# Where the first output tile's wo product is summed, when its head sums are read, and how the last output tile is cut

## The chip, the core and the metric

The kernel runs on one core of a Trainium2 chip. Five engines work side by side, each on its own instructions in its own order: TensorE (PE; its weight loads are listed as PEld), VectorE (DVE), ScalarE (ACT), GpSimd (POOL) and SyncE (SP), which here only issues transfers. They wait for one another through semaphores. The metric is device time in microseconds (us); lower is better. The kernel before takes 1537.7 us, the median of three runs from 1535.82 to 1538.98.

## What is computed

```python
mod = silu(c) @ w_mod                       # six rows of 640: sa, ca, ga, sb, cb, gb
h = layernorm(x) * (1 + ca) + sa            # x: 2048 x 640
q = h @ wq                                  # 32 heads of 128
p = softmax(q @ k_cache.T / sqrt(128))      # per head, 2048 keys
o = p @ v_cache
x = x + ga * (o @ wo)                       # o: 2048 x 4096, wo: 4096 x 640
h = layernorm(x) * (1 + cb) + sb
x1 = h + shift(gelu(layernorm(h) @ w1)) @ w2      # four groups of columns, shifted by 1, -1, 2, -2 tokens
h2 = gelu(layernorm(x1) @ w3) @ w4                # 640 -> 1728 -> 640
out = x + gb * (x1 + h2)
```

All inputs and the output are bf16; sums are in f32.

## The kernel before

The 2048 tokens are 16 tiles of 128. **Attention** runs over 512 steps `s`, head by head and in a head tile by tile (`h, j = divmod(s, 16)`). In a step PE multiplies the queries of tile `j` with all 2048 keys into the four banks of `Sps`, in two halves of 1024 columns (`qk`, L357 and L15). DVE copies each half to `negS`, negated and scaled, and keeps its minimum (L699). POOL takes the smaller of the two (L704), ACT the exponential of the row into a slot of `ring` (L707). The exponentials have to be transposed before they can be multiplied with the values: most of them by a DMA on SP for three steps at a time (a trio; `transpose`, L286), a few on PE (`t_piece`, L324, copied back by ACT, L331). Ten steps later (`PVD`) PE multiplies them with the values and a column of ones (`pv`, L371, 8 matmuls per half), and ACT copies the sums of two steps out of PSUM (L684). Four steps behind that POOL divides by the last column (L548, L555) and stores the result of four steps to `o_scratch` in DRAM (L562). So the loop has 526 rounds: steps 512 to 521 have no scores, only values.

`load_ot` (L604) reads `o_scratch` back for two tiles and a range of heads, transposed, into `OTj`, which lies in `hTx` for even pairs and in `negS` for odd ones. It is a DMA on SP's queue, so it takes its turn among the trios. Pair 0 (tiles 0 and 1) is read in three parts cut at `OTC = [0, 12, 31, 32]`: heads 0 to 11 in step 496, heads 12 to 30 in step 510 behind the last trio, head 31 in step 513. Each of the three lists the keys `HTK` (the old content of `hTx`) as written, so each waits for the landing of the part before. In step 513, SP also gets pair 1 in two halves of 16 heads, with the first four tiles of `x` (L612) between them; at step 522 the rest of `x`.

**The wo product** of tile 0 (`y0`, L643) is summed in the banks `Oaug` and `QPp`, that of tile 1 (`y1`, which calls `a_pe` on `Sps[:, 0:1024]`, L632) beside it; a head is one matmul of 512 and one of 128 columns. The table `TAIL` places pieces of them in the loop, behind the `pv` of a half step: in steps 506 to 511 (`Y0S = NG - 6`) one head of tile 0 per half step; in step 512 heads 0 to 7 of tile 1; in step 516 heads 8 to 11 of tile 1 and then heads 12 to 30 of tile 0. Behind the loop follow head 31 of tile 0, heads 12 to 31 of tile 1, and the other tiles by `a_pe` (tiles 2 to 5 in two halves of 16 heads, `a_two`). PE works strictly in this order: an instruction that waits holds up all that is listed behind it.

For each tile DVE then multiplies by `ga` (L757), adds `x` (L759), takes layernorm statistics (L749, L751; the root on POOL, L742, L744), modulates (L765, L768) and normalizes (L779); SP transposes the result (L785). The **MLP parts** follow with products L822 (w1), L885 (w2), L900 (w3) and L949 (w4), interleaved by a list.

The **last output tile** (tile 15, `e_last`) is worked in two halves of 320 columns: 14 matmuls each (L932) into two banks of the same `Sps` half, then on DVE a multiplication by `gb` (L915) and an addition (L918), then a store on SP (L921). `e_op` does the other tiles whole (L949; DVE L953, L955, L957; store L959). `ybank` hands out the two halves of `Sps` in turn.

`G.op` and `G.dma` record an operation with the keys that it reads (`r`) and writes (`w`); the waits are worked out from them, in the order of the program's text.

```python
Y0S = NG - 6
TAIL = {(s, z): [(y0, 2 * (s - Y0S) + z, 2 * (s - Y0S) + z + 1)] for s in range(Y0S, NG) for z in range(2)}
TAIL[(NG, 1)] = [(y1, 0, 8)]
TAIL[(NG + 4, 1)] = [(y1, 8, OTC[1]), (y0, OTC[1], OTC[2])]
```

Of the kernel before, what the change touches and what calls it, by code (L numbers as in the profile page):

```python
# [123 lines left out]
def bass_adaLN_cond__mha_block_cached__mixer_s_mlp__prompt_kernel(  # L124
# [21 lines left out]
    with ExitStack() as es:  # L146
# [9 lines left out]
        if True:  # L156
            with ExitStack() as es1:
# [445 lines left out]
                def load_ot(pr, h0=0, h1=H, part=0):  # L603
                    G.dma("sync", lambda e: e.dma_start_transpose(  # L604
                        OTj[pr % 2][:, 2 * h0:2 * h1, :], o_scr[pr, :, h0:h1].rearrange("q h z d -> q (h z d)")),
                          ("ot", pr % 2, part), r=[("osd", pr // 2, hh) for hh in range(h0, h1)],
                          w=[("OT", pr % 2, i) for i in ([part] if pr == 0 else (part, 2)[:part + 1] if h1 - h0 < H else range(3))]
                          + ([("OTa", 0)] if pr == 2 and part == 0 else [])
                          + (HTK if pr == 0 else NEG if pr == 1 and part == 0 else []))

                def load_xt(c0, c1):
                    G.dma("sync", lambda e: e.dma_start(  # L612
                        xt[:, 4 * c0:4 * c1], x2d[c0 * 512:c1 * 512, :].rearrange("(t p) d -> p t d", p=128)),
                        ("xt", c0), w=[("x1", t) for t in range(4 * c0, 4 * c1)] + ringk(XT0 + 4 * c0 * D, XT0 + 4 * c1 * D))

                OTC = [0, 12 * H // 32, H - 1, H]
                yn = [0]

                def ybank():
# [3 lines left out]
                def a_pe(j, b=None, parts=(0, 1, 2), hs=None):  # L623
                    if b is None:
                        b = ybank()
                    pr, z = divmod(j, 2)
                    h0, h1 = hs or (OTC[parts[0]], OTC[parts[-1] + 1])

                    def f(t):
                        for c0, cw in NC2:  # L630
                            for hh in range(h0, h1):
                                ins = t.matmul(YB[b][:, c0:c0 + cw], OTj[pr % 2][:, 2 * hh + z, :], wo[:, hh, c0:c0 + cw],  # L632
                                               start=(hh == 0), stop=(hh == H - 1))
                        return ins
                    G.op("tensor", f, r=[("OT", pr % 2, i) for i in parts] + [("OTa", pr % 2)] + ["wo", "woz", "wo4"],
                         w=[("S", b)] + ([("Sb", 2), ("Sb", 3)] if b == 1 else []))
                    return b

                def y0(h0, h1):
                    def f(t):  # L640
                        for jb, (c0, cw) in enumerate(NC2):
                            for hh in range(h0, h1):
                                ins = t.matmul(JB[jb][:, 0:cw], OTj[0][:, 2 * hh, :], wo[:, hh, c0:c0 + cw],  # L643
                                               start=(hh == 0), stop=(hh == H - 1))
                        return ins
                    G.op("tensor", f, r=[("OT", 0, i) for i in range(3) if OTC[i] < h1 and h0 < OTC[i + 1]] + [("OTa", 0), "wo", "woz", "wo4"],
                         w=[("J", 0), ("J", 1)])
# [7 lines left out]

                YB = [Sps[:, 0:1024], Sps[:, 1024:2048]]
                LAG = 4
                Y0S = NG - 6
                TAIL = {(s, z): [(y0, 2 * (s - Y0S) + z, 2 * (s - Y0S) + z + 1)] for s in range(Y0S, NG) for z in range(2)}
                TAIL[(NG, 1)] = [(y1, 0, 8)]  # L660
                TAIL[(NG + 4, 1)] = [(y1, 8, OTC[1]), (y0, OTC[1], OTC[2])]
                for s in range(NG + PVD + LAG):
                    h, j = divmod(s, NQT)
                    g_ = s - PVD
# [38 lines left out]
                    if s < NG:  # L703
                        G.op("gpsimd", lambda g, r8=r8: g.tensor_scalar(  # L704
                            out=nm[:, r8:r8 + 1], in0=nm0[:, r8:r8 + 1], scalar1=nm1[:, r8:r8 + 1], scalar2=None, op0=ALU.min),
                            r=[("nmh", 0, r8), ("nmh", 1, r8)], w=[("nm", r8)])
                        G.op("scalar", lambda a, s=s, r8=r8: a.activation(  # L707
                            ring[:, PSL[s], :], negS[:, s % 3, :], ACT.Exp, bias=nm[:, r8:r8 + 1], scale=-1.0),
                            r=[("negS", s % 3), ("nm", r8)], w=slot(PSL[s]))
                        for fn, *args in LATE.get(s, ()):  # L710
                            fn(*args)
                        if s in last_of:
                            transpose(last_of[s])
                        if j == 2 and h >= 1 and h + 1 < H:
                            load_k(h + 1)
                        if h + 1 == H and j in (0, NQT - 2):
                            i = int(j > 0)
                            load_ot(0, OTC[i], OTC[i + 1], i)
                        if j == (6 if h else 11) and h + 2 < H:
                            load_wq(h + 2)  # L720
                        if s == 9 and H > 1:
                            load_k(1)
                        if j == PVD + 1 and h + 1 < H:
                            load_v(h + 1)
# [117 lines left out]

                for i in range(NQT):
                    if i < NQT - 2:
                        b = (y0(OTC[2], H) or 0) if i == 0 else a_pe(1, 0, (1, 2)) if i == 1 else a_two(i) if i in (2, 3, 4, 5) else a_pe(i)
                    if i == NQT - 3:
                        for z in range(2):
                            G.op("gpsimd", lambda g, z=z: g.memset(us[:, :, z * SQ:z * SQ + 4], 0.0), w=[("usz", z)] + OT0K)  # L848
                    if i % 2 == 1 and (i + 3) // 2 < NQT // 2:
                        load_ot2((i + 3) // 2)  # L850
                    if i == 1:
                        G.dma("sync", lambda e: e.dma_start(w1, B_w1.rearrange("(k p) n -> p k n", p=128)), "w1", w=["w1"] + KVK)
                        G.dma("sync", lambda e: e.dma_start(w2, B_w2.rearrange("(k p) n -> p k n", p=128)), "w2", w=["w2"] + NEG)
                    if i < NQT - 2:
                        a_s1(i, b)
                    if 1 <= i:
                        a_s2(i - 1)
                    if 2 <= i:
                        nrm_of(1, i - 2)
                    if i == NQT - 2:  # L860
                        b = a_mixed(i, [[(b_op, 0, 0)], [(b_op, 0, 1)], [(b_op, 0, 2)], [(b_op, 0, 3)]])
                        a_s1(i, b)
                    if i == NQT - 1:
                        b = a_mixed(i, [[(b_op, 0, 4)], [(b_op, 1, 0)], [(b_op, 1, 1)], [(b_op, 1, 2)]])
                        nrm_of(1, i - 1)
                        a_s1(i, b)
                        a_s2(i)
                        nrm_of(1, i)
# [38 lines left out]
                def e_last(j):  # L907
                    b = ybank()
                    g = (j // 4) % 2
                    u = j % 2  # L910
                    q0 = (j % 4) * 128
                    for i in range(2):
                        c0 = i * HD
                        G.op("tensor", lambda t, i=i: e_half(t, b, g, q0, i), r=["w4", "w4b", "w4z", ("gT", g)], w=[("S", b, i)] + ([("S", b)] if i == 0 else []))
                        G.op("vector", lambda v, i=i, c0=c0: v.tensor_mul(  # L915
                            out=tmp[:, u, c0:c0 + HD], in0=YB[b][:, i * 512:i * 512 + HD], in1=mod_bc[:, 3 * D + c0:3 * D + c0 + HD]),
                            r=[("S", b, i), "mod"], w=[("tmp", u, i)] + ([("tmp", u)] if i == 0 else []))
                        G.op("vector", lambda v, c0=c0: v.tensor_add(  # L918
                            out=ob[:, u, c0:c0 + HD], in0=tmp[:, u, c0:c0 + HD], in1=xb[:, j, c0:c0 + HD]),
                            r=[("tmp", u, i), ("xb", j)], w=[("ob", u, i)] + ([("ob", u)] if i == 0 else []))  # L920
                        G.dma("sync", lambda e, c0=c0: e.dma_start(out2d[j * 128:(j + 1) * 128, c0:c0 + HD], ob[:, u, c0:c0 + HD]),  # L921
                              ("outl", i), r=[("ob", u, i)], w=[("ol", i)])

                def e_base(j):
# [2 lines left out]
                    G.op("vector", lambda v: v.tensor_add(out=xb[:, j], in0=xb[:, j], in1=xt[:, j]),  # L927
                         r=[("xb", j), ("x1", j)], w=[("xb", j)])

                def e_half(t, b, g, q0, i):  # L930
                    for f_ in range(NFT):
                        ins = t.matmul(YB[b][:, i * 512:i * 512 + HD], gT[g][:, f_, q0:q0 + 128],  # L932
                                       w4[:, f_, i * HD:(i + 1) * HD], start=(f_ == 0), stop=(f_ == NFT - 1))
                    return ins

                def e_op(j):
# [42 lines left out]
                    run_fill((2, 1, 1, 1, 2, 2, 1)[j] if j < 7 else 2)  # L979
                nrm_of(2, NQT - 1)  # L980
                run_fill(len(fill))
                G.flush("sync", [("ob", 0), ("ob", 1), ("ob", 1, 0), ("ob", 1, 1)])
                G.emit()


# [26 lines left out]
```

## Time and profile before

| | us |
|---|---|
| median of three runs | 1537.7 |
| the profiled execution | 1537.76 |
| its span, first to last instruction | 1536.0 |
| PE busy | 1473.2 (96%) |
| DVE busy | 1370.5 (89%) |
| ACT busy | 1257.6 (82%) |
| POOL busy | 625.8 (41%) |
| queue 1 (SP's transfers), share of 16 DMA engines | 100.7% |
| score steps end (last score matmuls) | 1210 |
| last `pv` matmuls end | 1239.6 |
| wo product of tile 15 ends | 1374.6 |
| last DVE operation ends | 1533.9 |

A busy share is a mean over stages that are limited by different things: in the score steps DVE works without a gap (its minimum of a half, 1222 ns, comes 1024 times), from 1240 us on PE does. The stretch of the edit lies between the two, from 1187 to 1263 us, where one stage runs out and the next has to be fed by transfers; the other edit touches the last 4 us. A matmul's listed length contains its way through the array, so the length of a stream of them is read from one start to another.

### The profile page before, as it was taken

How to read it: one execution, taken by the hardware profiler on the slowest of the kernel's cores; microseconds unless marked ns; L12 is line 12 of the kernel's file. 1: busy time of each engine (PE TensorE's matmuls, PEld its weight loads, DVE VectorE, ACT ScalarE, POOL GpSimd, SP SyncE). 2: the span in 40 equal slices, each digit the busy share in tenths (PEclk: the TensorE clock that was granted, in tenths of full speed). 3: DMA queues.
4: the chain of work that ended last, by engine and by line, in shares of the span. 5: the costliest groups of instructions: out<-in, count | busy, mean ns of one | idle time of the engine just before them, and what ended most of it. 6: DMA issues, size and time to landing. Idle time of an engine off the chain costs nothing.

```text
span 1536.0 us, 32447 instructions
## 1 busy us (share of the span) xinstructions
PE 1473.2 (96%) x13449; PEld 916.9 (60%) x12664; DVE 1370.5 (89%) x2424; ACT 1257.6 (82%) x1182; POOL 625.8 (41%) x1402
## 2 busy tenths in 40 slices
PE   6899999999999999999999999999999899999999
PEld 3466666666666666666666666666666565554545
DVE  8899999999999999999999999999999546668425
ACT  6999999999999999999999999999999600034230
POOL 1244444444444444444444444444444433333000
PEclk9999999999999999999999999999999999999999
DMA  9999999999999999999999999999999997624100
GB/s 331 244 231 252 231 250 235 236 234 248 243 247 242 239 241 237 246 234 249 231 251 235 244 232 250 232 239 235 246 233 243 231 242 165 142 74 116 35 22 35
DMA packets 1155088, 330.29 MB, mean 215 GB/s; under 512 B 1132986, under 2 KB 1149562, under 8 KB 1154938
## 3 DMA queue, kind: packets, MB, share of 16 engines
q1 hardware_dynamic: 1146448, 307.09, 100.7%
q0 software_dynamic: 6144, 16.79, 3.6%
q10 hardware_dynamic: 2346, 4.34, 0.8%
q8 instruction: 103, 1.69, 0.5%
q14 instruction: 47, 0.39, 0.1%
HBM read 43.48 MB, written 19.40 MB: 41 GB/s over the span
## 4 chain that ended last, share of the span: by engine, by line
ACT 62%; PE 19%; DVE 11%; DMA 4%; issue 3%; POOL 1%; SPq 0%; POOLq 0%; DVEq 0%
ACT ring L707 50%; DVE negS L699 10%; PE Sps L632 8%; ACT ring L331 4%; PE Sps L949 4%; ACT Of L684 3%; ACT kv L308 3%; DMA ring<-ring 2%; PE Oaug L900 2%; PE QPp L900 2%; PE Sps L885 1%; DMA ring<-in_A_x_dram 1%; PE PTp L371 1%; DMA kv<-Of 0%; DMA hTx<-o_scratch 0%
## 5 line engine op out<-in xcount | busy, mean ns | idle before, releaser
L699 DVE TENSOR_SCALAR_CACHE_REDUCE negS<-Sps 128x1024 f32<-128x1024 f32 x1024 | 1173.9, 1222 | 10.5 <-PE Sps L15 9.8
L707 ACT ACTIVATE ring<-negS,small 128x2048 bf16<-128x2048 f32 x512 | 1085.8, 2243 | 3.3 <-POOL small L704 3.2
L371 PEld LDWEIGHTS PTp<-kv,ring 128*128 128x128 bf16 x8192 | 557.4, 98 | 302.1 <-issue 75.7
L371 PE MATMUL PTp<-kv,ring 128*128 128x129 bf16 x8192 | 645.7, 221 | 11.4 <-DMA ring<-ring 10.4
L15 PE MATMUL Sps<-kv 128*128 128x512 bf16 x1007 | 383.0, 380 | 9.1 <-DVE negS L699 5.3
L704 POOL TENSOR_SCALAR small<-small 128x1 f32<-128x1 f32 x512 | 146.1, 285 | 598.1 <-DVE negS L699 598.0
L357 PE MATMUL Sps<-kv 128*128 128x512 bf16 x958 | 370.7, 387 | 14.5 <-DVE negS L699 2.4
L555 POOL TENSOR_SCALAR On<-Of,small 128x128 bf16<-128x128 f32 x512 | 190.1, 372 | 13.0
L357 PEld LDWEIGHTS Sps<-kv 128*128 128x128 bf16 x1024 | 98.3, 96 | 133.0 <-DVE negS L699 92.7
L684 ACT COPY Of<-PTp 128x259 f32<-128x259 f32 x256 | 153.3, 599 | 19.8 <-PE PTp L371 19.8
L548 POOL TENSOR_TENSOR small<-Of,small 128x4 f32<-128x4 f32 x128 | 133.1, 1040 | 18.4 <-ACT Of L684 18.3
L562 POOL DMA_DIRECT2D o_scratch<-On x128 | 103.8, 811 | 40.8 <-POOL On L555 37.2
L301 PE MATMUL Oaug<-hTx,kv 128*128 128x512 bf16 x254 | 96.3, 381 | 4.1 <-DMA kv<-in_A_wq_dram 2.4
L301 PE MATMUL QPp<-hTx,kv 128*128 128x512 bf16 x263 | 98.5, 382 | 1.1 <-ACT ring L331 0.8
L830 ACT ACT_TABLE_LOAD x1 | 1.3, 1283 | 109.9 <-POOL hTx L848 109.9
L699 DVE DVE_READ_ACCUMULATOR negS<-Sps 128x1 f32 x1024 | 87.2, 85 | 0.0
L742 POOL TENSOR_SCALAR negS<-negS 128x1 f32<-128x1 f32 x48 | 24.2, 504 | 121.8 <-DVE negS L751 121.8
L632 PE MATMUL Sps<-wo,negS 128*128 128x128 bf16 (+1 forms) x503 | 70.1, 298 | 0.5
L953 DVE TENSOR_TENSOR ring<-Sps,ring 128x640 f32<-128x640 f32 x15 | 12.4, 824 | 59.5 <-PE Sps L949 59.5
L331 ACT COPY ring<-QPp 128x512 f32<-128x512 f32 x78 | 63.8, 818 | 0.8 <-PE QPp L324 0.8
L331 ACT COPY ring<-Oaug 128x512 f32<-128x512 f32 x78 | 63.9, 819 | 0.0
L632 PE MATMUL Sps<-wo,hTx 128*128 128x512 bf16 (+1 forms) x441 | 60.8, 298 | 0.4
(108 smaller groups left out, 1053.1 us busy)
## 6 DMA issues: line engine op xcount, KB each, us to landing
kv<-in_A_v_cache_dram SPq DMA_DIRECT2D x32, 512.0 KB, 5.2
o_scratch<-On POOLq DMA_DIRECT2D x128, 128.0 KB, 5.6
kv<-in_A_wq_dram SPq DMA_DIRECT2D x32, 160.0 KB, 3.6
wo<-in_A_wo_dram SPq DMA_DIRECT2D x1, 5120.0 KB, 21.7
ring<-in_A_x_dram SPq DMA_DIRECT2D x5, 640.0 KB, 4.7
ring<-in_w_mod_dram SPq DMA_DIRECT2D x5, 640.0 KB, 8.6
out_dram<-wo SPq DMA_DIRECT2D x15, 160.0 KB, 1.8
ring<-ring SPq DMA_TRANSPOSE x144, 9.8
```

The source lines that it names most:

```text
L15: return t.add_instruction(mybir.InstMatmult(name=t.bass.get_next_instruction_name(), ins=[t.lower_ap(rhs), t.lower_ap(lhsT)], outs=[t.low ...
L301: G.op("tensor", lambda t: t.matmul(JB[jb], wq[:, hb, q, :], hT[:, q, cc * 512:(cc + 1) * 512], start=(q == 0), stop=(q == KT - 1)), r=[(" ...
L331: G.op("scalar", lambda a: a.copy(dst, src), r=keys[-1:], w=[("PT", TSL[g], r)])
L357: ins = (t.matmul if c2 == 0 else partial(same_weights, t))(Sps[:, col:col + 512], QT[:, hb, j * 128:(j + 1) * 128], KTs[:, hb, col:col + ...
L371: ins = t.matmul(ob[:, 0:129], pt, Vaug[:, hb, kt, 0:129], start=(kt == 0), stop=(kt == NKT - 1))
L548: G.op("gpsimd", lambda g: g.tensor_tensor(out=rl[:, 4 * b:4 * b + 4], in0=Of[:].rearrange("p a z d -> p (a z) d")[:, 4 * b:4 * b + 4, 128 ...
L555: G.op("gpsimd", lambda g: g.tensor_scalar(out=On[:, b, z, :], in0=Of[:, 2 * b + z // 2, z % 2, 0:128], scalar1=rl[:, 4 * b + z:4 * b + z ...
L632: ins = t.matmul(YB[b][:, c0:c0 + cw], OTj[pr % 2][:, 2 * hh + z, :], wo[:, hh, c0:c0 + cw], start=(hh == 0), stop=(hh == H - 1))
L684: G.op("scalar", lambda a, p=p: a.copy(Of[:, p % 4].rearrange("p z d -> p (z d)")[:, 0:259], PO[:, (p % 2) * 512:(p % 2) * 512 + 259]), r= ...
L699: G.op("vector", lambda v, half=half, dst=dst, src=src, r8=r8: v.tensor_scalar(out=dst, in0=src, scalar1=-SCALE, scalar2=None, op0=ALU.mul ...
L704: G.op("gpsimd", lambda g, r8=r8: g.tensor_scalar(out=nm[:, r8:r8 + 1], in0=nm0[:, r8:r8 + 1], scalar1=nm1[:, r8:r8 + 1], scalar2=None, op ...
L707: G.op("scalar", lambda a, s=s, r8=r8: a.activation(ring[:, PSL[s], :], negS[:, s % 3, :], ACT.Exp, bias=nm[:, r8:r8 + 1], scale=-1.0), r= ...
```

## The change

- `OTC` becomes `[0, 16, 31, 32]`: pair 0 is read as heads 0 to 15, 16 to 30, and 31.
- The second of these reads is issued in step 504 (`j == NQT - 8`) instead of 510: on SP's queue it stands behind the trio of steps 501 to 503 and ahead of those of 504 to 506 and 507 to 509.
- Only the first part writes the keys `HTK`; the other two no longer wait for the part before.
- `Y0S = NG - 8`: tile 0's heads 0 to 15 are summed in steps 504 to 511, one per half step.
- In step 513, behind its `pv` and `t_piece`, stand heads 16 to 30 of tile 0 and heads 0 to 30 of tile 1; the pieces of steps 512 and 516 are gone. Behind the loop only head 31 of both tiles is left.
- `e_last` takes three pieces of 320, 192 and 128 columns, the third in the other half of `Sps`; each has its 14 matmuls, two DVE operations and a store. `e_half` becomes `e_part`.

```diff
-                          + (HTK if pr == 0 else NEG if pr == 1 and part == 0 else []))
+                          + (HTK if pr == 0 and part == 0 else NEG if pr == 1 and part == 0 else []))
...
-                OTC = [0, 12 * H // 32, H - 1, H]
+                OTC = [0, H // 2, H - 1, H]
...
-                Y0S = NG - 6
+                Y0S = NG - 8
                 TAIL = {(s, z): [(y0, 2 * (s - Y0S) + z, 2 * (s - Y0S) + z + 1)] for s in range(Y0S, NG) for z in range(2)}
-                TAIL[(NG, 1)] = [(y1, 0, 8)]
-                TAIL[(NG + 4, 1)] = [(y1, 8, OTC[1]), (y0, OTC[1], OTC[2])]
+                TAIL[(NG + 1, 1)] = [(y0, OTC[1], OTC[2]), (y1, 0, OTC[2])]
...
-                        if h + 1 == H and j in (0, NQT - 2):
+                        if h + 1 == H and j in (0, NQT - 8):
                             i = int(j > 0)
                             load_ot(0, OTC[i], OTC[i + 1], i)
...
-                        b = (y0(OTC[2], H) or 0) if i == 0 else a_pe(1, 0, (1, 2)) if i == 1 else a_two(i) if i in (2, 3, 4, 5) else a_pe(i)
+                        b = (y0(OTC[2], H) or 0) if i == 0 else a_pe(1, 0, (2,)) if i == 1 else a_two(i) if i in (2, 3, 4, 5) else a_pe(i)
...
-                    for i in range(2):
-                        c0 = i * HD
-                        G.op("tensor", lambda t, i=i: e_half(t, b, g, q0, i), r=["w4", "w4b", "w4z", ("gT", g)], w=[("S", b, i)] + ([("S", b)] if i == 0 else []))
...
+                    b2 = ybank()
+                    for i, (c0, cw, dst, key) in enumerate([(0, 320, YB[b][:, 0:320], ("S", b)), (320, 192, YB[b][:, 512:704], ("S", b, 1)),
+                                                            (512, 128, YB[b2][:, 0:128], ("S", b2))]):
+                        G.op("tensor", lambda t, dst=dst, c0=c0, cw=cw: e_part(t, dst, g, q0, c0, cw), r=["w4", "w4b", "w4z", ("gT", g)], w=[key])
+                        G.op("vector", lambda v, c0=c0, cw=cw, dst=dst: v.tensor_mul(
+                            out=tmp[:, u, c0:c0 + cw], in0=dst, in1=mod_bc[:, 3 * D + c0:3 * D + c0 + cw]),
+                            r=[key, "mod"], w=[("tmp", u, i)] + ([("tmp", u)] if i == 0 else []))
+                        G.op("vector", lambda v, c0=c0, cw=cw: v.tensor_add(
+                            out=ob[:, u, c0:c0 + cw], in0=tmp[:, u, c0:c0 + cw], in1=xb[:, j, c0:c0 + cw]),
...
-                def e_half(t, b, g, q0, i):
+                def e_part(t, dst, g, q0, c0, cw):
                     for f_ in range(NFT):
-                        ins = t.matmul(YB[b][:, i * 512:i * 512 + HD], gT[g][:, f_, q0:q0 + 128],
-                                       w4[:, f_, i * HD:(i + 1) * HD], start=(f_ == 0), stop=(f_ == NFT - 1))
+                        ins = t.matmul(dst, gT[g][:, f_, q0:q0 + 128], w4[:, f_, c0:c0 + cw], start=(f_ == 0), stop=(f_ == NFT - 1))
```

## The prediction

> **What bounds the kernel now.** I read the shares and the chain of waits first, then the timelines of TensorE (PE) and of the DMA queue of SyncE (SP) where the edited lines run. Until 1206 us the chain is VectorE's (DVE) minimum over the scores; behind 1211 us it is almost only PE, with one long DMA in it:
>
> ```profile
> 1206.17 9.81 DMA ring<-ring
> ...
> 1220.37 7.22 DMA hTx<-o_scratch
> ...
> 1227.63 6.26 PE Oaug L643 x19
> 1233.89 1.06 PE QPp L643 x19
> ...
> 1262.78 8.64 PE Sps L632 x63
> ```
>
> Columns are start, length, what. L643 is `y0` (output tile 0 times wo, a 512- and a 128-column matmul per head), L632 is `a_pe` (the same for tile 1, here called `y1`, and later tiles); a whole tile of 32 heads takes 8.64 us, plus 0.05 of issue. The second read of head sums (L604, heads 12 to 30) is on the chain: PE waits for it. PE in order of time:
>
> ```profile
> 1192.84 0.63 PE L371 MATMUL PTp<-kv,ring 128*128 128x129 bf16 x8
> 1193.77 0.38 PE L15 MATMUL Sps<-kv 128*128 128x512 bf16 x1 [0.30 <-DVE negS L699]
> ...
> 1197.88 0.38 PE L643 MATMUL Oaug<-wo,hTx 128*128 128x512 bf16 x1
> ...
> 1210.08 0.38 PE L15 MATMUL Sps<-kv 128*128 128x512 bf16 x1
> ...
> 1211.04 1.10 PE L371 MATMUL PTp<-kv,ring 128*128 128x129 bf16 x16
> 1211.97 2.33 PE L632 MATMUL Sps<-wo,hTx 128*128 128x512 bf16 x16
> 1214.14 0.63 PE L371 MATMUL PTp<-kv,ring 128*128 128x129 bf16 x8
> ...
> 1216.02 0.64 PE L371 MATMUL PTp<-kv,ring 128*128 128x129 bf16 x8 [0.33 <-DMA ring<-ring]
> ...
> 1220.41 1.03 PE L632 MATMUL Sps<-wo,hTx 128*128 128x512 bf16 x7
> 1227.63 6.26 PE L643 MATMUL Oaug<-wo,hTx 128*128 128x512 bf16 x19 [6.19 <-DMA hTx<-o_scratch]
> ...
> 1234.79 4.85 PE L371 MATMUL PTp<-kv,ring 128*128 128x129 bf16 x80
> ...
> 1239.75 5.60 PE L632 MATMUL Sps<-wo,hTx 128*128 128x512 bf16 x40
> 1245.18 17.55 PE L632 MATMUL Sps<-wo,negS 128*128 128x512 bf16 x126
> ```
>
> Three things are to be seen: PE stands 6.19 us before 1227.63; the 40 matmuls of tile 1 (20 heads) come after that wait; and the first `y0` of the loop (step 506) runs at 1197.88 without waiting. The price of a head comes from the 40: 1245.18 - 1239.75 = 5.43 us for 20 heads, 0.2715 each. The 19 heads after the wait took 6.26 + 1.06 less an overlap, 1227.63 to 1234.79 = 7.16 us, where 19 x 0.2715 = 5.16: 2.0 us lost. The reason is the granted clock, here by windows (length, PE busy with its count, the other engines; then the clock; a view of PE alone has the clock third):
>
> ```profile
> 1221.50:1227.60 6.10, 0.00 (x0) 0.00 (x0) 0.00 (x0) 0.00 (x0) 0.00 (x0) 0.78 1.11 261
> ...
> 1532.07:1535.48 3.41, 0.73 (x6) 0.29 (x3) 1.63 (x4) 0.00 (x0) 0.00 (x0) 1.00 0.29 96
> 1535.48:1535.90 0.42, 0.00 (x0) 0.00 (x0) 0.00 (x0) 0.00 (x0) 0.00 (x0) 0.50 0.00 0
> ...
> 26.81:30.23 3.42, 1.90 (x14) 1.00 0.98 240
> ```
>
> It falls during the wait and is 0.50 again only at the very end of the program.
>
> SP works off its queue in order, nearly without a gap (start, length, queue; below it the wait list, and the time from issue to landing of the transposes that start at 1187.21, 1228.88 and 1235.13):
>
> ```profile
> 1187.21 5.03 SPq L604 DMA_TRANSPOSE hTx<-o_scratch  x1
> 1192.33 27.99 SPq L286 DMA_TRANSPOSE ring<-ring  x4
> 1220.37 8.46 SPq L604 DMA_TRANSPOSE hTx<-o_scratch  x2
> 1228.88 5.58 SPq L604 DMA_TRANSPOSE negS<-o_scratch  x1
> ...
> 1235.13 5.99 SPq L604 DMA_TRANSPOSE negS<-o_scratch  x1
> 1241.22 0.53 SPq L612 DMA_DIRECT2D ring<-in_A_x_dram  x1
> 1245.38 12.06 SPq L604 DMA_TRANSPOSE hTx<-o_scratch  x2
> ...
> SPq L109 <- DMA hTx<-o_scratch: 2.0, 1, 2.0
> ...
> hTx<-o_scratch SPq DMA_TRANSPOSE x1, 8.2
> ...
> negS<-o_scratch SPq DMA_TRANSPOSE x1, 7.6
> ...
> negS<-o_scratch SPq DMA_TRANSPOSE x1, 9.2
> ```
>
> The four trios cost 7.0 us of queue each, and the read of heads 12 to 30 stood behind all four.
>
> **Part by part. The wait at 1227.63 goes.** The read of heads 16 to 30 now stands ahead of the last two trios. SP: the first read (now 16 heads; 12 took 5.03, and 16 heads of another tile 5.58 to 5.99) ends near 1193.1, two trios 1207, the read is issued there. At 7.2 to 9.2 us it lands at 1214 to 1216. PE gets there (step 513, behind the values of steps 512 and 513, which take 0.93 + 1.40 us) not before 1213.4 + what the loop has lost; below that is 1216.7. So no wait, and the clock stays up: 6.19 + 2.0 us go. The 0.33 us ahead of 1216.02 goes as well: in its place stands the block of 15 heads of tile 0 and 31 of tile 1, 46 x 0.2715 = 12.5 us. Four heads of tile 0 (12 to 15) leave the stretch behind the loop for steps 504 to 507, 4 x 0.2715 = 1.09 us. The 19 heads of tile 1 that move from 1240 us into the block cost the same there. Removed: 6.19 + 2.0 + 0.33 + 1.09 = **9.6 us**.
>
> **What the moved reads delay.** The last two trios are issued near 1212 and 1219 in place of 1206.17 and 1213, and land (9.81 us in the chain) at 1222 and 1229. Behind the block PE wants them at 1229.2 and 1233.6. Hidden; without the block in front they would cost the 6 us. The wait of 2.0 us on SP goes, since the last read no longer waits for the landing of the one before it. So tile 2's two reads start at about 1227 and 1233.5 and land by 1235 and 1243.
>
> **A wait is added in step 504.** `y0` now starts two steps earlier, behind the eight matmuls of 1192.84, which leave PE at 1193.3 (8 at some 0.06 us). It needs the first read. That landed at 1187.21 + 8.2 = 1195.4 with 12 heads; with 16 I put it a third of its 5.03 us of queue at most, nothing at least, later (0 to 1.7), and take 1.0, the order of the difference to 5.99: 1196.4. PE so stands **3.1 us** (2.1 to 3.8). All behind it on PE wait: the second score half of step 504, hence DVE, ScalarE's exponentials and everything to the loop's end. It isn't made up: with `y0` in them the 14 halves between 1193.77 and 1210.08 took 16.31 us, 1.165 each, and those with `y0` are set by PE without a gap; the four halves of steps 504 and 505 join them for some 0.1 to 0.2 us. Added: **3.3 us**. SP is not held up: its trios are behind by then anyway.
>
> **Does this stall drop the clock?** In the rows a stretch of 3.41 us with 1.90 us of PE work kept it at 1.00 and one with 0.73 lost it. A stall of 3.1 us leaves between 0.3 and 1.9 us of work in the emptier of the two stretches that it touches, by where it falls. If it drops, some 3.4 us of loop run at half speed: 1.7 us more (the trace's own case: 2.0). I take no drop, for the stall that shows one is twice as long. The Trainium skill ("TensorE: Matmul & The Clock Gate", Part 1: The HAM clock gate) says that the clock falls after at least one whole idle window of about 3.4 us, the windows running freely; by that 3.1 us costs nothing and the sum stands. The row of 1532.07 speaks against the strict form of it, having 0.73 us of work in its window, which is why the drop is a rival below.
>
> **What comes after.** PE's way from 1211.04 to 1262.78 loses 9.6 and gains 3.3: tile 2 starts at 1238.9 instead of 1245.18, its second half at 1243.2, with its heads landed by 1243; tile 3 follows, tile 4 starts at 1256.5. Tile 4's two reads waited on SP until 1245.38 for tile 1's matmuls; now they go out near 1240.5, straight behind the transfer of the row of 1241.22, and their 12.06 us of queue end near 1252.5, where the two halves of tile 4 want them at 1256.5 and 1260.8. From there PE is the chain to the end, and the **6.3 us** stay.
>
> **Last tile in three pieces.** DVE:
>
> ```profile
> 1531.00 0.82 DVE L957 TENSOR_TENSOR wo<-ring 128x640 bf16<-128x640 f32 x1
> 1531.74 0.48 DVE L915 TENSOR_TENSOR ring<-Sps,mod_bc 128x320 f32<-128x320 f32 x1
> 1532.26 0.49 DVE L918 TENSOR_TENSOR wo<-ring 128x320 bf16<-128x320 f32 x1
> 1532.84 0.49 DVE L915 TENSOR_TENSOR ring<-Sps,mod_bc 128x320 f32<-128x320 f32 x1
> 1533.36 0.49 DVE L918 TENSOR_TENSOR wo<-ring 128x320 bf16<-128x320 f32 x1
> ...
> 1240.56 0.28 DVE L757 TENSOR_TENSOR ring<-QPp,mod_bc 128x128 f32<-128x128 f32 x1
> ```
>
> DVE, not PE, sets this end: it comes from the tile before without a gap, and waited only some 0.07 us for the second half. A start-to-start of 0.52 us for 320 columns and 0.31 for 128 gives 0.38 for 192. The first piece is over at 1532.78 as before; then 2 x 0.38 + 2 x 0.31 = 1.38 to 1534.16, where it was 1533.85: **0.3 us lost**. Bounds: 0.1 gained, if the third transfer, of 32 KB for 80, returns faster, to 0.5 lost.
>
> **Sum.** The profiled execution took 1537.76 us (its span 1536.0), the median of three is 1537.7. 1537.76 - 9.6 + 3.3 + 0.3 = **1531.8 us**, and as much against the median.
>
> **Rivals.** (1) The stall in step 504 drops the clock: 1.7 us more, 1533.5. For it, the row of 1532.07; against it, a stall shorter than the stretch of 3.41 us. (2) The stall is short or absent, the first read landing as early as before: PE gains up to 9.6, but then waits for the second half of tile 2's heads, which cannot land before 1244.3 less the 2.0 us of the SP wait; tile 4 starts at 1242.3 + 4.34 + 8.69 = 1255.3, 7.5 us earlier: 1530.6. For it only the small growth of the read. (3) The DMA engines and not SP's wait set tile 2's reads: they land at 1244.3 as before, and tile 4 starts at 1257.3: 1532.6. (4) Slower: the block of 92 matmuls stands in front of the values of the last eight steps, and all of them wait if the read of heads 16 to 30 is late. Behind its landing PE still has 12.5 + 4.4 + 4.9 + 0.6 = 22.4 us (block, values of steps 514 to 516, the 80 matmuls, the two last heads) up to tile 2, which began at 1245.18; so it decides from a landing at 1222.5 on, 15.5 us after its issue. A landing after 20 us would give 1227 + 22.4 + 2.0 of clock = 1251.4, 6.2 us late: 1544.3. Against it, all rows of L604 land within some 10 us. A landing a few us late only eats the gain: at 1221 the time is 1536.3.
>
> **How the numbers follow.** Forecast with (3), which differs by less than 1 us: 0.55; (1) 0.25; (2) 0.12; (4) 0.08, half of it past the point of no gain. The range goes from 1530.2, just below (2), to 1534.4, above (1) with the stall at its upper bound. What differs by less than 0.2% (3.1 us) can't be told from no change here; faster thus means under 1534.6, which the first three give but for the far end of (1): 0.9; the same 0.06; slower 0.04.
>
> **What would show it.** In the profile after: a PE wait of about 3 us for `hTx<-o_scratch` at 1193 us in the loop, at a clock of 1.00 behind it; no wait ahead of the block of 92 matmuls at about 1217; the last 80 values matmuls ending near 1238; tile 4 at 1256.5; the last DVE piece 1.38 us after the first. Wrong are my reasons if that first wait is missing, if the block stands waiting for its read, if the trios are waited for behind it, or if the gain of 6.3 us is gone by the MLP.

## The result, and the profile after

The changed kernel takes 1530.88 us, the median of six runs (1529.45 to 1532.75); the kernel before, beside it, 1537.5 (1534.63 to 1540.31). The ratio is 0.9959 with a 95% interval of 0.9945 to 0.9973, so 4.2 to 8.5 us of gain: faster, by more than the 0.2% named in the prediction, and 0.9 us under the forecast of 1531.8.

The profiled execution took 1530.71 us, its span 1528.9. Its span is 7.1 us shorter than that of before, but 1.6 us of this were there before the first edited instruction of PE: the first score matmul of step 504, just ahead of it, starts at 1190.81 us, before at 1192.39. A distance between two starts of one profile is free of that. From this matmul to the first one of tile 4 ("the stretch" from here on) before took 1262.78 - 1192.39 = 70.4 us, and the changed kernel 1255.41 - 1190.81 = **64.6 us**. The rest, to the end of the span, took 273.2 and 273.5.

The chain of waits of the changed kernel (start, length, what) through the edited part:

```profile
1185.66 8.63 DMA hTx<-o_scratch
1194.34 0.39 PE Oaug L643
...
1216.31 3.24 PE Oaug L643 x15
1219.55 0.84 PE QPp L643 x15
1220.39 8.42 PE Sps L632 x62
...
1232.96 4.68 PE PTp L371 x80
...
1237.91 32.21 PE Sps L632 x233
```

The DMA on the chain is now the first read, not the second. Behind it PE runs without a gap. The timeline of PE, same kernel:

```profile
1191.26 0.63 PE L371 MATMUL PTp<-kv,ring 128*128 128x129 bf16 x8
1194.34 0.39 PE L643 MATMUL Oaug<-wo,hTx 128*128 128x512 bf16 x1 [2.45 <-DMA hTx<-o_scratch]
...
1194.85 0.63 PE L15 MATMUL Sps<-kv 128*128 128x512 bf16 x1
...
1196.67 0.63 PE L357 MATMUL Sps<-kv 128*128 128x512 bf16 x1
...
1198.60 0.38 PE L357 MATMUL Sps<-kv 128*128 128x512 bf16 x1
...
1216.15 3.40 PE L643 MATMUL Oaug<-wo,hTx 128*128 128x512 bf16 x15
...
1228.64 0.63 PE L371 MATMUL PTp<-kv,ring 128*128 128x129 bf16 x8
...
1232.80 4.84 PE L371 MATMUL PTp<-kv,ring 128*128 128x129 bf16 x80
...
1238.02 17.55 PE L632 MATMUL Sps<-wo,negS 128*128 128x512 bf16 x128
1255.41 17.55 PE L632 MATMUL Sps<-wo,hTx 128*128 128x512 bf16 x128
```

Three things answer to the prediction. The wait of 6.19 us ahead of the 19 heads is gone, and the block starts at 1216.15 without one. A new wait of 2.45 us stands ahead of the first `y0` in step 504. And behind it score matmuls last 0.63 us instead of 0.38 until 1198.6. That is the clock, by two windows of 3.41 us (length, PE busy, the clock):

```profile
1191.49:1194.90 3.41, 0.96 (x11) 0.99 1.26 253
1194.90:1198.31 3.41, 3.41 (x22) 0.51 1.28 290
```

From one score half to the next it is 2.05 and 1.93 us in this time, where 1.17 is the rule: 1.64 us for the clock. The wait itself made the half of step 504 3.81 us long instead of 1.14 to 1.16: 2.65. (The wait is listed from the listed end of the matmuls before it, hence 2.45.) In all the loop from step 504 to its last score half takes 21.84 us (1190.81 to 1212.65) for 17.48 before (1192.39 to 1209.87), 4.4 lost; from there to tile 4 it takes 42.8 for 52.9, 10.1 won.

SP's queue in the same profile:

```profile
1185.66 5.50 SPq L604 DMA_TRANSPOSE hTx<-o_scratch  x1
1191.26 12.25 SPq L286 DMA_TRANSPOSE ring<-ring  x2
1203.55 5.41 SPq L604 DMA_TRANSPOSE hTx<-o_scratch  x1
1209.06 14.08 SPq L286 DMA_TRANSPOSE ring<-ring  x2
1223.29 1.17 SPq L604 DMA_TRANSPOSE hTx<-o_scratch  x1
1224.51 4.71 SPq L604 DMA_TRANSPOSE negS<-o_scratch  x1
...
1229.90 5.92 SPq L604 DMA_TRANSPOSE negS<-o_scratch  x1
```

The second read goes out at 1203.55 and is there (7.5 us) before PE asks; the last two trios, landing 9.8 and 10.4 us after their issue, are on time as well. The last tile on DVE:

```profile
1524.72 0.48 DVE L915 TENSOR_TENSOR ring<-Sps,mod_bc 128x320 f32<-128x320 f32 x1
1525.24 0.49 DVE L918 TENSOR_TENSOR wo<-ring 128x320 bf16<-128x320 f32 x1
1525.64 0.35 DVE L915 TENSOR_TENSOR ring<-Sps,mod_bc 128x192 f32<-128x192 f32 x1
1526.03 0.36 DVE L918 TENSOR_TENSOR wo<-ring 128x192 bf16<-128x192 f32 x1
1526.31 0.28 DVE L915 TENSOR_TENSOR ring<-Sps,mod_bc 128x128 f32<-128x128 f32 x1
1526.62 0.29 DVE L918 TENSOR_TENSOR wo<-ring 128x128 bf16<-128x128 f32 x1
```

2.19 us from the first of these to the end of the last (before 2.11), and 1.99 more to the end of the span (before 2.15): 4.18 for 4.26.

### The profile page after: what moved, and what is told of

Same layout as the page of the kernel before. It is cut to its first block, busy times and chain, and to the rows that moved or that the text cites. A ratio compares the mean times of both kernels' runs of the same rounds, so it can differ in the third digit from the quotient of the medians.

```text
span 1528.9 us, 32717 instructions
## 1 busy us (share of the span) xinstructions
PE 1489.2 (97%) x13702; PEld 918.8 (60%) x12678; DVE 1370.9 (90%) x2426; ACT 1258.5 (82%) x1182; POOL 627.0 (41%) x1402
## 4 chain that ended last, share of the span: by engine, by line
ACT 70%; PE 21%; DVE 4%; DMA 3%; issue 2%; SPq 1%; POOL 0%; DVEq 0%
ACT ring L706 57%; PE Sps L632 9%; ACT ring L331 4%; ACT Of L683 4%; ACT kv L308 4%; PE Sps L948 3%; DVE negS L698 3%; PE Oaug L899 2%; PE QPp L899 2%; PE PTp L371 1%; PE Sps L884 1%; DMA ring<-ring 1%; DMA kv<-in_A_wq_dram 1%; ACT hTx L473 1%; SPq L222 1%
## 5 line engine op out<-in xcount | busy, mean ns | idle before, releaser
L706 ACT ACTIVATE ring<-negS,small 128x2048 bf16<-128x2048 f32 x512 | 1112.7, 2355 | 5.3 <-POOL small L703 4.8
L357 PE MATMUL Sps<-kv 128*128 128x512 bf16 x1024 | 396.0, 387 | 8.1 <-DVE negS L698 3.6
L15 PE MATMUL Sps<-kv 128*128 128x512 bf16 x1024 | 389.2, 380 | 0.0
L683 ACT COPY Of<-PTp 128x259 f32<-128x259 f32 x256 | 181.6, 710 | 4.5 <-PE PTp L371 4.5
L301 PE MATMUL Oaug<-hTx,kv 128*128 128x512 bf16 x315 | 119.4, 381 | 4.8 <-DMA kv<-in_A_wq_dram 3.3
L301 PE MATMUL QPp<-hTx,kv 128*128 128x512 bf16 x325 | 121.3, 379 | 0.9 <-ACT ring L331 0.8
L331 ACT COPY ring<-QPp 128x512 f32<-128x512 f32 x78 | 73.1, 937 | 0.0
L331 ACT COPY ring<-Oaug 128x512 f32<-128x512 f32 x78 | 72.9, 935 | 0.0
```

The source lines that it names most:

```text
L15: return t.add_instruction(mybir.InstMatmult(name=t.bass.get_next_instruction_name(), ins=[t.lower_ap(rhs), t.lower_ap(lhsT)], outs=[t.low ...
L301: G.op("tensor", lambda t: t.matmul(JB[jb], wq[:, hb, q, :], hT[:, q, cc * 512:(cc + 1) * 512], start=(q == 0), stop=(q == KT - 1)), r=[(" ...
L331: G.op("scalar", lambda a: a.copy(dst, src), r=keys[-1:], w=[("PT", TSL[g], r)])
L357: ins = (t.matmul if c2 == 0 else partial(same_weights, t))(Sps[:, col:col + 512], QT[:, hb, j * 128:(j + 1) * 128], KTs[:, hb, col:col + ...
L683: G.op("scalar", lambda a, p=p: a.copy(Of[:, p % 4].rearrange("p z d -> p (z d)")[:, 0:259], PO[:, (p % 2) * 512:(p % 2) * 512 + 259]), r= ...
L706: G.op("scalar", lambda a, s=s, r8=r8: a.activation(ring[:, PSL[s], :], negS[:, s % 3, :], ACT.Exp, bias=nm[:, r8:r8 + 1], scale=-1.0), r= ...
```

## The experiments

All are edits of the changed kernel (the runs called again repeat a kernel). The theory: the order of the reads took away the wait and the cold clock behind it, and the price is the early `y0`, by its wait and by the clock. The stretch is read from each profile, and so is the distance from the same matmul to the end of the span, since what is won ahead of tile 4 can be lost behind it; times are medians, ratios are to the kernel before.

| run | stretch, us | to the end, us | time, us | ratio, 95% interval |
|---|---|---|---|---|
| before | 70.4 | 343.6 | 1537.5 | |
| changed | 64.6 | 338.1 | 1530.88 | 0.9959 (0.9945 to 0.9973) |
| changed, again | 64.8 | 338.2 | 1532.6 | 0.9962 (0.9947 to 0.9977) |
| e1: `y0` from step 506 | 62.7 | 336.9 | 1528.62 | 0.9949 (0.9937 to 0.9962) |
| e2: `y0` from step 505 | 62.0 | 336.7 | 1529.11 | 0.9952 (0.9940 to 0.9964) |
| e2 again (e11) | 63.0 | 338.2 | 1529.07 | 0.9942 (0.9927 to 0.9958) |
| e3: the wait filled | 63.3 | 337.0 | 1530.12 | 0.9962 (0.9946 to 0.9978) |
| e4: second read behind the trios | 75.7 | 349.2 | 1541.79 | 1.0035 (1.0021 to 1.0048) |
| e5: block in step 516 | 68.1 | 341.8 | 1534.3 (one run) | |
| e6: keys of the reads kept | 63.2 | 337.3 | 1530.01 (one run) | |
| e7: last tile in two halves | 61.6 | 335.5 | 1528.61 (one run) | |
| e8: e2, block begins with tile 1 | 62.3 | 335.6 | 1531.46 | 0.9964 (0.9952 to 0.9977) |
| e9: e1, first read of 12 heads | 65.3 | 338.8 | 1529.9 | 0.9960 (0.9948 to 0.9973) |

**The order of the reads (e4).**

```diff
-                        if h + 1 == H and j in (0, NQT - 8):
+                        if h + 1 == H and j in (0, NQT - 2):
```

> Edit: the changed kernel with the read of heads 16 to 30 back in step 510, behind the last two trios on SP. Theory (the order of the read is what pays): it is issued 14 us later and lands near 1225 on the scale of the changed kernel, PE waits 8.7 us ahead of the block and loses 2.0 to the clock: 75.3 us for the stretch, 10.7 us more time than the changed kernel and 4 to 5 more than before the change. Rival (what pays is the new place of tile 1's heads and the steps 504 and 505): 64.6, no loss.

PE's timeline in e4, the block's first matmuls:

```profile
1223.47 6.19 PE L643 MATMUL Oaug<-wo,hTx 128*128 128x512 bf16 x15 [10.22 <-DMA hTx<-o_scratch]
```

A wait of 10.22 us, and 15 heads at half clock. The stretch is 75.7 us where the theory had 75.3, and the kernel is slower than before the change. That the two numbers agree so well is luck: from the last score half to tile 4 it took 55.9 us for 42.8, 13.2 more where 10.7 was expected, and in the loop PE waited only 2.01 us and kept its clock, 2.1 less. With everything else of the change in place, the read's turn on SP decides between a gain and a loss.

**The wait and the clock in step 504 (e1, e2, e3).** e1 sets `Y0S = NG - 6` and begins the block with head 12 (`(y0, 12, OTC[2])`); e2 takes `NG - 7` and 14. e3 puts ten matmuls into the wait:

```diff
+                def busy(n):
+                    def f(t):
+                        for _ in range(n):
+                            ins = t.matmul(JB[0], wo[:, 0, 0:128], wo[:, 1, 0:512], start=True, stop=True)
+                        return ins
+                    G.op("tensor", f, r=["wo"], w=[("J", 0)])
+                TAIL[(Y0S, 0)] = [(busy, 10)] + TAIL[(Y0S, 0)]
```

> Edit: tile 0 is summed from step 506 on (heads 0 to 11, as before the change), heads 12 to 30 in the block of step 513; reads and the rest as in the changed kernel. Measured on PE from the first score matmul of step 504 to the first matmul of tile 4: before 70.4 us, changed 64.6. Theory (the wait in step 504, 2.6 us, and the clock drop behind it, about 1.65, are on the path): both go, four heads (1.1) come back into the block, so 61.4 us and 3.2 us less time than the changed kernel. Rival (the wait is absorbed, since the transfers set the end): 64.6 to 65.7, no gain.

> Edit: tile 0 is summed from step 505 on (heads 0 to 13), heads 14 to 30 in the block. Theory: the first read lands 3.5 us after the first score matmul of step 504, and the first y0 is now due 3.2 us after it: a wait of 0.3 us, no clock drop, two heads (0.5) back in the block: 61.2 us for the stretch that took 64.6. Rival (absorbed): 64.6 or more. A second rival (the wait is set by something other than the read's landing and moves along with y0): again a wait of 2.5 us and 64.6.

> Edit: the changed kernel with ten matmuls of 512 columns (2.15 us, their result is overwritten) ahead of the first y0 in step 504, where PE waits anyway. Theory (the clock drop is a cost of its own): the wait for the read shrinks to about 0.4 us, the end of the wait stays, the granted clock stays at 1.00, the stretch takes 62.9 us instead of 64.6. Rival (the drop costs nothing, since DVE or the transfers set the pace there): 64.6. Were the wait not for the read, it would be 2.15 us longer: 66.8.

The waits of PE, first e1, then e2, then e3:

```profile
1200.48 0.64 PE L371 MATMUL PTp<-kv,ring 128*128 128x129 bf16 x8 [0.73 <-DMA ring<-ring]
1212.20 4.28 PE L643 MATMUL Oaug<-wo,hTx 128*128 128x512 bf16 x19 [0.29 <-DMA hTx<-o_scratch]
```

```profile
1212.17 3.84 PE L643 MATMUL Oaug<-wo,hTx 128*128 128x512 bf16 x17 [0.84 <-DMA hTx<-o_scratch]
```

```profile
1194.32 0.39 PE L643 MATMUL Oaug<-wo,hTx 128*128 128x512 bf16 x1 [0.61 <-DMA hTx<-o_scratch]
```

In e1 and e2 the wait in step 504 and the drop are gone, and the stretch is 1.9 and 2.6 us shorter. The theory had 3.2 and 3.4: with the loop earlier, PE comes to other transfers too early, for 0.73 us to the trio of steps 498 to 500 and for 0.29 and 0.84 to the second read. So the wait was on the path, but not all of it comes back, and more is lost behind the stretch. The next wait of PE in e2, ahead of tile 6:

```profile
1270.58 17.56 PE L632 MATMUL Sps<-wo,negS 128*128 128x512 bf16 x128 [1.05 <-DMA negS<-o_scratch]
```

In e1 this wait is 0.33 us; the changed kernel has none there. SP issued the read in question at 1258.97 us in e2 and at 1258.56 in the changed kernel: it didn't come earlier with PE. Of the 2.6 us that e2 won up to tile 4, 1.3 reached the end of the span.

In e3 the score halves behind the wait are 1.17 us apart again and the clock stays; the stretch is 1.3 us shorter, though its read landed 0.3 us later against step 504 than the changed kernel's (3.85 us behind its first score matmul, for 3.53). The drop alone therefore cost about 1.6 us, as the distances between score halves say. All this is read from profiles: the intervals of the ratios of the changed kernel, e1, e2 and e3 overlap.

**The block as cover (e5).**

```diff
-                TAIL[(NG + 1, 1)] = [(y0, OTC[1], OTC[2]), (y1, 0, OTC[2])]
+                TAIL[(NG + 4, 1)] = [(y0, OTC[1], OTC[2]), (y1, 0, OTC[2])]
```

> Edit: the changed kernel with the block of 92 matmuls in step 516, where part of it stood before, instead of 513. Theory (the block is the work that covers the wait for the late trios): PE reaches the values of step 514 some 2.6 us before their trio lands, so the stretch from the first score matmul of step 504 to tile 4 takes 67.2 us for 64.6, or 68.9 if the clock falls there too. Rival (PE has slack elsewhere behind the loop): 64.6.

```profile
1218.00 0.64 PE L371 MATMUL PTp<-kv,ring 128*128 128x129 bf16 x8 [2.08 <-DMA ring<-ring]
```

That is PE's wait for the trio of step 504 in e5; the clock fell behind it as well. 68.1 us, between the two numbers expected; from the last score half to tile 4 it took 46.6 us for 42.8. In the changed order the last trios are late, and the block in front of them hides it.

**The keys of the reads (e6).**

```diff
-                          + (HTK if pr == 0 and part == 0 else NEG if pr == 1 and part == 0 else []))
+                          + (HTK if pr == 0 else NEG if pr == 1 and part == 0 else []))
```

> Edit: the changed kernel, but all three reads of pair 0 write the keys HTK again, so each waits for the landing of the one before it. The prediction put the 2.0 us of SP's wait down to these keys and counted their end for tile 2's reads. Theory now: in the new order the part before has long landed (the second near 1211 us, the third is issued at 1223), so SP shows no gap and the stretch stays at 64.6 us. Rival (the keys are what freed SP): a gap of up to 2 us on SP ahead of the read of head 31, tile 2's second read landing 2 us later, still within its slack of 3.6 us: the stretch the same, the gap seen.

SP in e6, around the read of head 31:

```profile
1209.09 13.45 SPq L286 DMA_TRANSPOSE ring<-ring  x2
1222.64 1.21 SPq L604 DMA_TRANSPOSE hTx<-o_scratch  x1
1223.90 4.43 SPq L604 DMA_TRANSPOSE negS<-o_scratch  x1
```

0.10 us between the trios and the read: no gap. The keys matter only where one read follows another at once: in e4, which has the old order without the keys, the two reads also stood without a gap (5.71 us for both, where before they took 8.46 with the wait). The stretch of 63.2 us was not expected, and it has another reason: PE waited longer in step 504 than in the changed kernel and kept its clock. The wait, and then two windows of 3.41 us, laid by the places where the clock changes in this profile (length, PE busy, the clock):

```profile
1194.87 0.22 PE L643 MATMUL QPp<-wo,hTx 128*128 128x128 bf16 x1 [2.88 <-DMA hTx<-o_scratch]
1189.25:1192.66 3.41, 2.60 (x28) 1.00 1.10 242
1192.66:1196.07 3.41, 1.21 (x13) 1.00 1.26 253
```

The record of the 512-column matmul ahead of this 128-column one is missing from the trace; with its 0.22 us the wait is some 2.66 us and the work in the lower window some 1.43.

**The last tile (e7).** `e_last` and `e_half` as before the change.

> Edit: the changed kernel with the last tile in two halves again. In the profiles, from the start of DVE's first multiplication of that tile to the end of its last addition: before 2.11 us, changed 2.19; from there to the end of the span 2.15 and 1.99. Theory (by these rows the three pieces are worth nothing: two small DVE operations more, one smaller transfer last): again 2.1 and 2.1 us, the sum within 0.15 us of the changed kernel's 4.18. The prediction had 0.3 us more for the three pieces; rival (they gain, as the last transfer is smaller): the sum 0.3 us or more above 4.18.

From DVE's first piece to the end 2.12 us, from there to the end of the span 2.08: 4.20, against 4.18. Over the eleven profiles with three pieces the sum lies between 4.12 and 4.19. By this the three pieces are worth less than 0.1 us, which no time can show. (Its short stretch, 61.6, comes from a first read that landed early: a wait of 1.06 us and no drop.)

**Closing the small waits (e8, e9).** e8 is e2 with `[(y1, 0, OTC[1]), (y0, 14, OTC[2]), (y1, OTC[1], OTC[2])]` in the block; e9 is e1 with `OTC = [0, 12, H - 1, H]` and the block in the same order.

> Edit: y0 from step 505 on as in e2, and in the block heads 0 to 15 of tile 1 stand first (they need only the first read), then heads 14 to 30 of tile 0, then 16 to 30 of tile 1. Theory: the wait of 0.84 us for the second read ahead of the block is covered by 4.3 us of matmuls; 61.2 us for the stretch where e2 took 62.0. Rival (PE waits for something else as much later, tile 2's second read above all): 62.0.

> Edit: the first read is again of 12 heads, the second of 19 (still ahead of the last two trios), y0 from step 506 on, and the block begins with heads 0 to 11 of tile 1. Theory: the wait of 0.73 us that e1 had for the trio of steps 498 to 500 came from the longer first read and goes, its wait of 0.29 us for the second read is covered: 61.5 us where e1 took 62.7. Rival (the trio is late for another reason): 62.4.

PE, e8 and then e9, second half of tile 2:

```profile
1240.55 13.21 PE L632 MATMUL Sps<-wo,negS 128*128 128x512 bf16 x94 [1.29 <-DMA negS<-o_scratch]
```

```profile
1243.45 14.90 PE L632 MATMUL Sps<-wo,negS 128*128 128x512 bf16 x94 [2.16 <-DMA negS<-o_scratch]
```

Both lost the small waits that they were made against, and tile 2 begins 43.5 and 43.9 us after step 504's first matmul, for 44.6 in e2 and 47.2 in the changed kernel. Both then wait for the second read of tile 2's heads, and in e9 the clock fell behind that wait. For e8 this is what its rival had named. For e9 neither number held: the wait for the trio went, as the theory had it, but the stretch took 65.3 us, for the new wait and the clock. So these reads are the next bound: in e8 SP's list has no gap of more than 0.1 us from the first read, at 1186.06 us, up to this one, which goes out at 1230.31. No run moved them, so what could be won there stays open.

**Once more, side by side (e10, e11).**

> The changed kernel once more, for its time beside e11 on one chip, and for whether its wait in step 504 drops the clock in this execution too. Theory (the clock is judged in stretches of 3.4 us that lie anywhere to the program): a wait of 2.5 to 2.9 us, dropped or not; the stretch 64.6 us if dropped, 63.1 if not.

> e2 once more beside e10. Theory: no wait above 0.4 us in the loop, 62.0 us for the stretch, the median 1 to 3 us under e10's. Rival (e2's lead was chance): medians within 0.5 us.

The changed kernel waited 2.60 us and dropped its clock (64.8 us). e2 waited 0.74 us in step 505 and 1.11 ahead of the block (63.0), more than its theory allowed. The medians are 3.5 us apart here and were 1.8 apart before (1530.88 and 1529.11), and the intervals of the ratios overlap in both cases. The profiles don't settle it either. In e11, too, PE waited ahead of tile 6:

```profile
1273.28 17.56 PE L632 MATMUL Sps<-wo,negS 128*128 128x512 bf16 x128 [1.29 <-DMA negS<-o_scratch]
```

From step 504 to the end e2 and e11 took 336.7 and 338.2 us, the changed kernel 338.1 and 338.2: a lead of 1.3 us in one pair and none in the other. e11 had reached step 504 2.3 us sooner than e10, ahead of any difference on PE. "From step 505" has the better medians, but that it is the better version is not shown.

## Why the prediction was right

- **The wait ahead of the 19 heads, and what goes with it, 9.6 us.** Right in mechanism and nearly in size: behind the loop 10.1 us went. (If each of the two listed waits, of 6.19 and 0.33 us, was some 0.2 us longer by distances between starts, as that of step 504 is, that makes 0.4 of the difference: an estimate.) e4 brings the wait back by the read's place alone.
- **The delayed trios, hidden.** Right, and e5 prices the cover: with the block three steps later 2.08 us of wait and a clock drop, 3.8 us behind the loop. The 6 us that the prediction named for no cover at all were not tried.
- **SP's wait of 2.0 us.** It went, but the cause was half right: with the new order it would have gone with the keys in place (e6). Neither put tile 2's reads on the path of the changed kernel; in e8 and e9 they are.
- **The wait in step 504.** Forecast as 3.1 us, measured 2.65: the read of 16 heads landed 8.6 us after its issue, where 9.2 was assumed. Over the executions with `y0` from step 504 and nothing put into the wait, it is listed as 1.06 us (e7) to 2.60 (the changed kernel again), and is some 2.66 in e6.
- **The clock.** Here the forecast took the wrong case: it held the stall too short for a drop, and the profile shows the drop of the first rival, at its price (1.64 us for 1.7). e3 shows it to be a cost of its own. It does not come in every execution: it came in the changed kernel, in its repetition and in e5, and not in e4 (2.01 us) or in e6, whose wait is longer than the changed kernel's. What tells them apart in these profiles is where the wait falls. In the clock records of each of the thirteen profiles, all changes lie whole multiples of 3.41 us apart, so windows can be laid over every wait. In the changed kernel the whole wait lies in one window, which has 0.96 us of PE work; in e6 an edge at 1192.66 us cuts the wait, and the emptier window has some 1.43. Between step 504 and tile 4, every window of the changed kernel and its edits that the clock fell behind had at most 1.34 us of work (that of e5's second wait), and those with 1.43 or more kept it. That puts the line near 1.4 us of 3.41, an estimate from few rows which no run tested.
- **The last tile, 0.3 us lost.** Mis-sized: the DVE operations are 0.08 us longer in all, not 0.3. A multiplication began 0.40 us after the addition of 320 columns before it, not 0.52; by that, the second half of the kernel before, at 0.58, had stood 0.18 us rather than 0.07. From the last addition to the end of the span it was 0.16 us less, as expected of a smaller last transfer, though e7, with the larger one, had 2.08 for the 1.99.
- **The sum.** The stretch gained 5.8 us where 6.3 was forecast: a shorter wait in step 504 and 0.5 more behind the loop, less the clock. That the time came out 0.9 us under the forecast is in part luck. The drop that the forecast left out should have put it 1.6 above; the misses of the other terms and the 1.6 us that the profiled execution was ahead at step 504 made up for it. The median gained 6.6 us, not the 5.8 less 0.3 behind tile 4 that the two profiles show, and the difference lies within the spread between runs.

The strict rule of the Trainium skill that the prediction weighed ("TensorE: Matmul & The Clock Gate", Part 1) doesn't hold here: the window before the drop had 0.96 us of PE work in it, so a window need not be idle throughout. That the windows run freely agrees with the traces: the edge next to the wait lies 0.6 us behind step 504's first score matmul in the changed kernel (1191.41 us by the clock records, 0.08 ahead of the window listed above) and 1.7 behind it in e6 (1192.66).

## What to carry to other kernels

Where one queue issues both what feeds the next matmuls and what feeds later ones, the order on that queue can be worth as much as the work itself: the same read ahead of two 7 us transposes or behind them was 11 us of this kernel. Work moved up to cover a wait has needs of its own; ask for each moved piece when its operand lands. Starting it a step later took the wait out of the loop here, but look where PE then arrives too early: of what was won up to tile 4, half was left at the end in one profile and nothing in the other. A PE wait of 2 to 3 us can cost another 1.6 us through the clock, in one execution and not in the next, by how it lies across the windows of 3.41 us.

## What had not been expected

Executions of the same instructions reached the first score matmul of step 504 anywhere between 1189.83 us (e4) and 1193.67 (the changed kernel again), though nothing before it on PE was edited. That spread of 3.8 us is as large as most differences tested here. Distances inside a profile showed what the times could not, provided that they reach to the end of the span.
